# A decode layer on one core: five engine programs without a closing block

## The chip, the cores and the metric

The kernel runs on one core of a Trainium2 chip. A core has five engines with a program each: TensorE (PE, with its weight loads shown as PEld), VectorE (DVE), ScalarE (ACT), GpSimd (POOL) and SyncE (SP). [...] SyncE computes nothing here; it issues nearly all transfers (DMAs) from HBM. The metric is the time of one execution in device microseconds (us), 680.14 as the median of three runs of the kernel before.

## The reference

One token goes through one transformer layer with conditioning. `c` gives six vectors (shift, scale and gate for attention and for the feed-forward part). Attention has 32 heads of 128 over a cache of 16384 positions; K and V are read in full, 268 MB in bf16, and everything else is small beside them.

```python
mod = (_silu(c) @ w_mod).reshape(c.shape[0], 6, 1, -1)
sa, ca, ga, sb, cb, gb = ...
h = _layernorm(x) * (1 + ca) + sa
x = x + ga * A(h, k_cache, v_cache, wq, wo)      # softmax(q k / sqrt(128)) v, then wo
h = _layernorm(x) * (1 + cb) + sb
x = x + gb * B(h, w_gate, w_up, w_down)          # (silu(h wg) * (h wu)) wd
```

## The kernel before

The heads go in 16 pairs. For each pair SyncE brings 8 MB of K into one half of the ring `kring` and 8 MB of V into `vbuf`. DVE multiplies K by the query (L554, L570) and folds the products (L559, L564, L576), PE sums what is left into scores (L544, L584), DVE and PE find the largest (L589, L593, L597), ACT takes the exponential (L601), PE weighs V (L518), ACT and PE gather the output (L524, L533, L537). A half of the ring is filled again once PE has read the scores out of it, and `vbuf` once PE has read V. At the front stand the modulation vectors and the queries (L378 to L484); at the end the output projection, the second layer norm and the feed-forward part (L663 to L775), with the weights brought into freed halves of the ring.

The order of work is written out by hand. `op` and `dma` append operations to a list (`dma` is the helper at L90, so that all transfers have that line); each names its engine and the operations that it needs. `emit` goes through the list once, gives each engine its operations in the order of the list, and puts a wait ahead of an operation where its engine does not yet know that what it needs is done. The middle pairs are loops on ACT, DVE and PE (L187, L191); SyncE's and GpSimd's programs have no loop. GpSimd does two operations in all: it fills `ones_bf` (L359) and makes the identity matrix `ident` (L360) that DVE reads at L413 and PE as weights later. The last transfers are the two halves of the output row, one from SyncE and one from ACT, and SyncE's last operation is `final_wait` (L779), which needs both.

Around this stand two handshakes of all five engines. The first belongs to the set-up of every program and has the line of the launch, L813: four engines drain and raise a semaphore, GpSimd gathers the four and releases them. Then each engine goes by a branch into its own part of a block (`nc.Block`, entered at L243), and when it has reached the end of its part it goes by a branch to the block's common end. There the same handshake is made again: drain, gather by GpSimd, release. These instructions have the line L243.

Of the kernel before, what the change touches and what calls it, by code (L numbers as in the profile page):

```python
# [37 lines left out]
class _Plan:  # L38
# [38 lines left out]
    def op(self, eng, fn, deps=(), name="", chan=None):  # L77
        o = _Op(eng, fn, list(deps), name, len(self.ops), self.loop.get(eng), chan)
        o.sig = chan is not None
        self.ops.append(o)  # L80
        return o
# [20 lines left out]
                need[k] = (d.chan, d.val)  # L102
        return need

    def emit(self, block):
        for o in self.ops:
            for d in o.deps:
                d.sig = True
                assert d.seq < o.seq, (o.name, d.name)
        per_eng = {e: [o for o in self.ops if o.eng == e] for e in self.ENGS}  # L110
        for e in self.ENGS:
            by_place = {}
            for o in per_eng[e]:
                if o.loop:
                    key, i, n = o.loop
                    by_place.setdefault((key, i), []).append(o)
            for (key, i), ops in by_place.items():
                first = by_place[(key, 0)]
                assert len(first) == len(ops), (key, i)
                for a, b in zip(first, ops):  # L120
                    a.sig = a.sig or b.sig
            for (key, i), ops in by_place.items():
                for a, b in zip(by_place[(key, 0)], ops):
                    b.sig = a.sig
            for o in per_eng[e]:
                if o.sig:
                    ch = o.chan if o.chan is not None else self.chans[e]
                    o.chan = ch
                    ch.count += ch.inc
                    ch.ops.append(o)  # L130
                    o.val = ch.count

        def issue(eng, o):
            ins = o.fn(eng)
            if o.sig:
                assert ins is not None, o.name
                ins.then_inc(o.chan.sem, o.chan.inc)

        def run(name, eng):
            known = {}  # L140
            ops = per_eng[name]
            at = 0
            while at < len(ops):
                o = ops[at]
                if o.loop is None:
                    for k, (ch, v) in self.needs(o).items():
                        if known.get(k, 0) < v:
                            eng.wait_ge(ch.sem, v)
                            known[k] = v
                    issue(eng, o)  # L150
                    at += 1
                    continue
                key, i, n = o.loop
                end = at
                while end < len(ops) and ops[end].loop and ops[end].loop[0] == key:
                    end += 1
                body = (end - at) // n
                rows = [ops[at + j * body:at + (j + 1) * body] for j in range(n)]
                assert (end - at) == body * n and all(x.loop[1] == j for j, r in enumerate(rows) for x in r)
                done = {}  # L160
                body_needs = []
                for b in range(body):
                    each = [self.needs(r[b]) for r in rows]
                    assert all(set(x) == set(each[1]) for x in each[1:]), rows[0][b].name
                    for k, (ch, v) in each[0].items():
                        if k not in each[1]:

                            assert ch.ops[v // ch.inc - 1].seq < ops[at].seq, rows[0][b].name
                            if known.get(k, 0) < v:
                                eng.wait_ge(ch.sem, v)  # L170
                                known[k] = v
                    waits = []
                    for k, (ch, v1) in each[1].items():
                        step = each[2][k][1] - v1
                        v0 = v1 - step
                        assert all(x[k][1] == v0 + j * step for j, x in enumerate(each) if j), (rows[0][b].name, [x[k][1] for x in each])
                        assert v0 > 0 and step >= 0
                        assert k not in each[0] or each[0][k][1] <= v0, rows[0][b].name
                        assert v0 % ch.inc == 0 and ch.ops[v0 // ch.inc - 1].seq < rows[0][b].seq, rows[0][b].name
                        if known.get(k, 0) >= each[-1][k][1]:  # L180
                            continue
                        if k in done and done[k][1] == step and done[k][0] >= v0:
                            continue
                        done[k] = (v0, step)
                        waits.append((ch, v0, step))
                    body_needs.append(waits)
                with eng.Fori(0, n) as it:  # L187
                    self.turn = it
                    for b in range(body):
                        for ch, v0, step in body_needs[b]:  # L190
                            eng.wait_ge(ch.sem, v0 if step == 0 else it * step + v0)  # L191
                        issue(eng, rows[0][b])
                    self.turn = None
                for k, (v0, step) in done.items():
                    known[k] = max(known.get(k, 0), v0 + (n - 1) * step)
                at = end

        @block.sync
        def _(e):
            run("sp", e)  # L200

        @block.scalar
        def _(e):
            run("act", e)

        @block.vector
        def _(e):
            run("dve", e)

        @block.tensor  # L210
        def _(e):
            run("pe", e)

        @block.gpsimd
        def _(e):
            run("pool", e)


def build(nc, A_x, A_k, A_v, A_wq, A_wo, B_wg, B_wu, B_wd, c_in, w_mod, out):
# [21 lines left out]

    es = ExitStack()
    with es:  # L243
        block = es.enter_context(nc.Block())
        plan = _Plan(nc, es)
        op, dma = plan.op, plan.dma
        POOL, ACT, DVE, PE = "pool", "act", "dve", "pe"
# [529 lines left out]
        d_outs = [dma(o_dst[0:2], o_row[31:33, :], "out0", deps=[o_or], name="dma_out0"),  # L777
                  dma(o_dst[2:4], o_row[95:97, :], "out1", deps=[o_or], name="dma_out1", eng="act")]
        op("sp", lambda e: e.nop(), deps=d_outs, name="final_wait")  # L779
        plan.emit(block)  # L780
    return plan


def bass_adaLN_cond__gqa_block_cached__swiglu_ffn__decode_kernel(
    nc: bass.Bass,
    A_x: bass.AP,
    A_k_cache: bass.AP,
    A_v_cache: bass.AP,
    A_wq: bass.AP,
    A_wo: bass.AP,  # L790
    B_x: bass.AP,
    B_w_gate: bass.AP,
    B_w_up: bass.AP,
    B_w_down: bass.AP,
    c: bass.AP,
    w_mod: bass.AP,
    out: bass.AP,
):
    build(nc, A_x, A_k_cache, A_v_cache, A_wq, A_wo, B_w_gate, B_w_up, B_w_down, c, w_mod, out)
# [28 lines left out]
```

## Time and profile before

| | us |
|---|---|
| Median of three runs | 680.14 |
| Lowest, highest | 679.78, 680.22 |
| Span of the profiled execution, first to last instruction | 678.3 |
| Median less span | 1.8 |
| DVE busy | 513.5 (76%) |
| PE busy | 362.0 (53%) |
| ACT busy, POOL busy | 46.4, 0.7 |
| Transfers | 428 GB/s, 99.2% of 16 engines' span |

The page gives no time of its own for the profiled execution beside its span, so the two are compared by the median. A view by line lists an instruction's engine (a `q` behind the name is the engine's sequencer, which handles drains, semaphores and branches), its operation, how often, its least, median and greatest length in ns, and the first and last start in us from the span's start. The timeline has start, length, engine, line and operation, and in brackets how long the engine was idle before and what released it. The chain of waits is followed back from the last computing instruction or issue, in order of time. The profile starts at the first instruction of the program, the handshake of L813, and ends with the last.

### The profile page before, as it was taken

The page shows a single profiled execution, that of the slowest core. Times are in us where ns is not written, and L with a number is a line of the kernel's source. Part 1 is how long each engine was busy: PE and PEld are TensorE (multiplying, and loading weights), DVE is VectorE, ACT ScalarE, POOL GpSimd, SP SyncE. Part 2 cuts the span into 40 slices and gives each one's busy share as a digit, 9 for nine tenths or more (in the row PEclk, how much of TensorE's full clock was granted, in tenths as well). Part 3 has the DMA queues.
Part 4 walks back from the last instruction along what each step waited for, and adds up shares of the span by engine and source line. Part 5 has one row for each costly group of instructions (what it writes and reads, how often), then busy time and mean ns, then how long its engine had stood idle before and what let it go on. Part 6 is the DMA issues. An engine that isn't in the chain of part 4 may idle for free.

```text
span 678.3 us, 5380 instructions
## 1 busy us (share of the span) xinstructions
PE 362.0 (53%) x2052; PEld 143.4 (21%) x2053; DVE 513.5 (76%) x186; ACT 46.4 (7%) x146; POOL 0.7 (0%) x6
## 2 busy tenths in 40 slices
PE   2520475755728174654818375562818465471676
PEld 1110122221312122221302122121212222130235
DVE  2189997959596896959597795959698695959812
ACT  1120000100000000000000010000000000000010
POOL 0000000000000000000000000000000000000000
PEclk9675565655657565565757555575756556575775
DMA  8999999999999999999999999999999999999997
GB/s 372 443 461 429 433 437 430 433 429 433 433 429 433 437 433 433 433 433 433 433 433 433 433 433 437 433 433 433 433 433 433 433 433 433 433 433 433 433 408 304
DMA packets 6355, 290.58 MB, mean 428 GB/s; under 512 B 714, under 2 KB 972, under 8 KB 1484
## 3 DMA queue, kind: packets, MB, share of 16 engines
q1 hardware_dynamic: 6340, 290.48, 99.2%
q8 instruction: 5, 0.08, 0.0%
q14 instruction: 2, 0.02, 0.0%
q10 hardware_dynamic: 8, 0.00, 0.0%
HBM read 290.47 MB, written 0.00 MB: 428 GB/s over the span
## 4 chain that ended last, share of the span: by engine, by line
DMA 49%; DVE 30%; issue 13%; PE 8%; SPq 0%; DVEq 0%
DMA kring<-in_A_k_cache_dram 45%; DVE kring L554 10%; PE psb L544 7%; DVE kring L559 6%; DVE kring L570 5%; DVE kring L576 5%; DMA kring<-in_B_w_down_dram 4%; DVE kring L564 3%; PE psb L584 1%; SPq L90 0%; DVE pm L589 0%; DVE nb L597 0%; PE psb L765 0%; DVEq L191 0%; DVEq L554 0%
## 5 line engine op out<-in xcount | busy, mean ns | idle before, releaser
L554 DVE TENSOR_TENSOR kring<-kring,qbc 128x16384 bf16<-128x16384 bf16 x28 | 243.2, 8687 | 96.4 <-DMA kring<-in_A_k_cache_dram 96.4
L544 PE MATMUL psb<-kring,ident 128*128 x448 | 197.6, 607 | 121.3 <-DVE kring L564 121.3
L559 DVE TENSOR_TENSOR kring<-kring 128x8192 bf16<-128x8192 bf16 x28 | 123.8, 4420 | 0.5
L544 PEld LDWEIGHTS psb<-kring,ident 128*128 128x128 bf16 x448 | 54.0, 120 | 249.0 <-issue 248.3
L518 PE MATMUL psb<-vbuf,PZ 128*8 128x512 bf16 x960 | 80.4, 509 | 0.0
L593 PE MATMUL psb<-d,bd_f 128*128 128x64 f32 x32 | 10.9, 446 | 118.8 <-ACT d L591 118.8
L564 DVE TENSOR_TENSOR kring<-kring 128x4096 bf16<-128x4096 bf16 x28 | 64.0, 2286 | 0.5
L570 DVE TENSOR_TENSOR kring<-kring,qbc 128x16384 bf16<-128x16384 bf16 x4 | 34.8, 8688 | 23.4 <-DMA kring<-in_A_k_cache_dram 23.4
L518 PEld LDWEIGHTS psb<-vbuf,PZ 128*8 128x8 bf16 x960 | 26.5, 107 | 58.5 <-issue 48.6
L584 PE MATMUL psb<-kring,ident 128*128 128x128 bf16 (+1 forms) x48 | 14.3, 463 | 44.2 <-DVE kring L576 44.2
L593 PEld LDWEIGHTS psb<-d,bd_f 128*128 128x128 f32 x32 | 8.0, 311 | 121.3 <-DVE pm L589 111.6
L576 DVE TENSOR_TENSOR kring<-kring 128x8192 bf16<-128x8192 bf16 (+2 forms) x12 | 31.7, 2645 | 0.3
L533 PEld LDWEIGHTS psb<-sel,acc_sb 128*128 128x128 f32 x128 | 28.5, 310 | 8.5 <-issue 4.3
L533 PE MATMUL psb<-sel,acc_sb 128*128 128x2 f32 x128 | 25.6, 322 | 1.4 <-ACT acc_sb L524 1.4
L524 ACT ACTIVATE acc_sb<-psb 128x512 f32<-128x512 f32 x16 | 9.6, 597 | 209.7 <-PE psb L518 209.7
L601 ACT ACTIVATE PZ<-psb,nb 64x256 bf16<-64x256 f32 x32 | 15.0, 469 | 64.8 <-DVE nb L597 64.6
L584 PEld LDWEIGHTS psb<-kring,ident 128*128 128x128 bf16 x48 | 5.6, 122 | 51.8 <-DVE kring L576 44.9
L591 ACT ACTIVATE d<-negid,pm 128x64 f32<-128x64 f32 x16 | 5.6, 348 | 154.3 <-DVE pm L589 154.3
L477 PE MATMUL psb<-vbuf,h_col 128*128 128x512 bf16 x39 | 11.2, 459 | 8.3 <-DMA vbuf<-in_A_wq_dram 8.3
L537 ACT ACTIVATE OT_sb<-psb 128x2 f32 (+1 forms) x16 | 2.8, 172 | 153.3 <-PE psb L533 153.3
L589 DVE TENSOR_REDUCE pm<-psb 128x1 f32<-128x256 f32 x16 | 6.7, 418 | 3.7 <-PE psb L584 3.7
L477 PEld LDWEIGHTS psb<-vbuf,h_col 128*128 128x128 bf16 x40 | 4.3, 116 | 15.5 <-DMA vbuf<-in_A_wq_dram 8.8
(105 smaller groups left out, 77.8 us busy)
## 6 DMA issues: line engine op xcount, KB each, us to landing
kring<-in_A_k_cache_dram SPq DMA_DIRECT2D x2, 4096.0 KB, 40.1
vbuf<-in_A_wq_dram SPq DMA_DIRECT2D x1, 5120.0 KB, 25.6
kring<-in_w_mod_dram SPq DMA_DIRECT2D x1, 4800.0 KB, 14.0
vbuf<-in_A_wo_dram SPq DMA_DIRECT2D x1, 4480.0 KB, 23.3
kring<-in_B_w_gate_dram SPq DMA_DIRECT2D x1, 2160.0 KB, 18.9
kring<-in_B_w_up_dram SPq DMA_DIRECT2D x1, 2160.0 KB, 23.7
kring<-in_B_w_down_dram SPq DMA_DIRECT2D x3, 640.0 KB, 25.0
vbuf<-in_A_wo_dram SPq DMA_DIRECT2D x1, 640.0 KB, 24.5
```

The lines of the kernel that those rows point to most:

```text
L477: last = e.matmul(q_ps[b][:, 0:512], lhsT=h_col[:, k:k + 1].broadcast_to([128, 128]), rhs=wq_v[:, k, g * 512:(g + 1) * 512], start=(k == 0 ...
L518: last = e.matmul(acc_ps[32 * s:32 * s + 8, :], lhsT=PZ[:, j, :], rhs=v_at(p)[:, 4 * j:4 * j + 4, :].rearrange("p t d -> p (t d)"), start= ...
L533: last = e.matmul(OT_ps[:, 0:2], lhsT=acc_sb[:, 128 * i:128 * (i + 1)], rhs=sel[:, i:8:4], start=(i == 0), stop=(i == 3))
L544: last = e.matmul(S_ps[:, 0:T2], lhsT=ident[:], rhs=kring[:, bass.ds(plan.slot(p), 1), :, d].rearrange("p o t -> p (o t)"), start=(d == 0) ...
L554: return e.tensor_tensor(out=kv4, in0=kv4, in1=q4, op=ALU.mult)
L559: o_f = op(DVE, lambda e: e.tensor_tensor(out=kv4[:, :, 0], in0=kv4[:, :, 0], in1=kv4[:, :, 1], op=ALU.add), deps=[o_m], name="fold%d_%d" ...
L564: return op(DVE, lambda e: e.tensor_tensor(out=lo[:, :, 0:QR], in0=lo[:, :, 0:QR], in1=lo[:, :, QR:QW], op=ALU.add), deps=[o_f], name="fol ...
L570: o = op(DVE, lambda e: e.tensor_tensor(out=kv, in0=kv, in1=qbc[:, p, :].unsqueeze(1).broadcast_to([128, KCUT[c + 1] - KCUT[c], 128]), op= ...
L576: o = op(DVE, lambda e, w=w: e.tensor_tensor(out=kv[:, :, 0:w], in0=kv[:, :, 0:w], in1=kv[:, :, w:2 * w], op=ALU.add), deps=[o], name="fol ...
L584: last = e.matmul(S_ps[:, a:b], lhsT=ident[:], rhs=kring[:, p % 2, a:b, d], start=(d == 0), stop=(d == 15))
L593: o_mx[p] = op(PE, lambda e: e.matmul(mx_ps[:, 0:64], lhsT=bd_f[:], rhs=d2[:], start=True, stop=True), deps=[o_d2, o_bd1, o_bd2, o_nb[p - ...
L601: o_exp[p] = op(ACT, lambda e, half=half, ps=ps: e.activation(out=PZ[ps, :, 4 * half:4 * half + 4], in_=S_ps[ps, 0:T2].rearrange("p (c i) ...
```

## The change

The block is no longer entered. SyncE's and GpSimd's operations are put straight into the main program, behind the first handshake. ACT, DVE and PE, whose programs have loops, are sent from the main program by a branch each into a body of their own, which stands alone and has no common end. With the block go its closing drain, gather and release on all five engines, and the branches to it. The waits and operations that `emit` makes for each engine are the same, in the same order, `final_wait` among them. All lines behind the edits stand 11 lines higher in the file after.

```diff
-    def emit(self, block):
+    def emit(self):
...
-        @block.sync
-        def _(e):
-            run("sp", e)
-
-        @block.scalar
-        def _(e):
-            run("act", e)
-
-        @block.vector
-        def _(e):
-            run("dve", e)
-
-        @block.tensor
-        def _(e):
-            run("pe", e)
-
-        @block.gpsimd
-        def _(e):
-            run("pool", e)
+        nc = self.nc
+        run("sp", nc.sync)
+        run("pool", nc.gpsimd)
+        looped = [(nc.scalar, "act"), (nc.vector, "dve"), (nc.tensor, "pe")]
+        for eng, name in looped:
+            nc.br("go_" + name, engines=[eng.engine])
+        for eng, name in looped:
+            with nc.body("go_" + name, valid_engines=[eng.engine]):
+                run(name, eng)
...
-        block = es.enter_context(nc.Block())
...
-        plan.emit(block)
+        plan.emit()
```

## The prediction

> **What bounds the kernel now.** I read the page first (shares, slices, queues), then the chain of waits in order of time, and last the instructions that the closing handshake itself left, line by line. The header and the first rows give the frame:
>
> ```profile
> span 678.3 us, 5380 instructions
> ...
> PE 362.0 (53%) x2052; PEld 143.4 (21%) x2053; DVE 513.5 (76%) x186; ACT 46.4 (7%) x146; POOL 0.7 (0%) x6
> ...
> DMA  8999999999999999999999999999999999999997
> ...
> q1 hardware_dynamic: 6340, 290.48, 99.2%
> q8 instruction: 5, 0.08, 0.0%
> q14 instruction: 2, 0.02, 0.0%
> HBM read 290.47 MB, written 0.00 MB: 428 GB/s over the span
> ```
>
> The reader is to see that no compute engine is full, that the transfers of queue 1 are (99.2% of what 16 engines can take), and that the two queues which carry instructions took no measurable share. The stream of K, V and weights from HBM sets the length, so between its first issue and its last landing an edit that issues no transfer and holds none up is worth nothing. What is left to win lies before the first issue and behind the last landing. The timeline and the chain show both ends:
>
> ```profile
> 0.74 0.07 issue
> ...
> 0.80 0.40 SPq L90 DMA_DIRECT2D kring<-in_w_mod_dram  x1
> ...
> 648.87 26.02 DMA kring<-in_B_w_down_dram
> 674.89 0.04 issue
> 674.94 1.06 PE psb L765 x21
> 676.00 0.02 issue
> 676.02 0.34 DVE qbc L774
> 676.36 0.02 issue
> 676.38 0.24 DVE o_row L775
> ...
> 676.65 0.33 SPq L90 DMA_DIRECT2D out_dram<-o_row  x1
> 676.66 0.26 ACTq L90 DMA_DIRECT2D out_dram<-o_row  x1
> ```
>
> The first columns are start and length in us. The last weights land at 674.9, the output row is ready at 676.6, its two halves are issued at 676.65. Everything after that is waiting for the output to land and the handshake. The instructions of the lines concerned follow (length in ns as least, median and most, then first and last start in us); L779 is the final wait, L243 the block whose end makes the handshake, L813 the handshake before the program:
>
> ```profile
> L779 SPq EVENT_SEMAPHORE  x1: 17/17/17, 677.8 to 677.8; - x1
> ...
> L243 POOLq EVENT_SEMAPHORE  x2: 17/17/17, 678.1 to 678.2; - x2
> L243 POOLq DRAIN  x1: 387/387/387, 1.0 to 1.0; - x1
> L243 PEldq DRAIN  x1: 363/363/363, 675.7 to 675.7; - x1
> L243 DVEq DRAIN  x1: 280/280/280, 676.4 to 676.4; - x1
> L243 ACTq DRAIN  x1: 241/241/241, 677.0 to 677.0; - x1
> L243 SPq COMPARE_BRANCH  x1: 33/33/33, 678.0 to 678.0; - x1
> L243 SPq DRAIN  x1: 7/7/7, 678.1 to 678.1; - x1
> L243 SPq EVENT_SEMAPHORE  x1: 17/17/17, 678.3 to 678.3; - x1
> L243 ACTq EVENT_SEMAPHORE  x1: 17/17/17, 678.3 to 678.3; - x1
> L243 DVEq EVENT_SEMAPHORE  x1: 21/21/21, 678.3 to 678.3; - x1
> L243 PEldq EVENT_SEMAPHORE  x1: 51/51/51, 678.3 to 678.3; - x1
> ...
> SPq L779 <- DMA out_dram<-o_row: 0.8, 1, 0.8
> SPq L243 <- PEq L243: 0.2, 1, 0.2
> ```
>
> Four engines drain while others still work or the output is in flight (1.0, 675.7, 676.4 and 677.0), so their drains cost nothing today. On the path are only SyncE's branch at 678.0, its drain, GpSimd's two semaphore instructions and the four releases at 678.3: the 0.2 us in the last row is SyncE's wait for the release.
>
> **The change, part by part.** The sum is made against this execution, whose page gives a span of 678.3; its own time is not listed. The median of the three runs is 680.14 (679.78 to 680.22), so 1.8 us of a run lie outside the span, and I carry them as a separate term.
>
> *The closing handshake goes.* Removed are five drains, GpSimd's gather and go and four releases, 11 instructions, and the branches to the common end. Of these the path holds the stretch from 678.0 to the end of the span: 678.3 - 678.0 = 0.3 us. With the rounding of both rows it is 0.25 to 0.4. What is late next: the landing of the output. SyncE waits for two semaphores at L779; one instruction of 17 ns is shown at 677.8 and then nothing of SyncE until the branch at 678.0. Either the branch carries the second wait and the 0.2 us are the other half of the output still in flight, or they are the way to the branch. In the first case they stay (the new program waits for both semaphores in one instruction, which would start at about 678.0); in the second they go too, and the gain is 0.5. I take the first: the two halves leave within 0.01 us of each other on two queues, but the branch is 33 ns long and no row shows SyncE needing 0.2 us from one control instruction to the next (its first issue follows the opening release by 0.07). So -0.3, between -0.25 and -0.5.
>
> *SyncE's and GpSimd's programs stand in the main program.* No DMA, no wait and no operation changes its order on any engine; set side by side, the two instruction lists differ on SyncE in the branch in and the branch out, on GpSimd the same. SyncE's transfers and GpSimd's memset and select are issued in the order they had. What can move is the way into the program:
>
> ```profile
> L813 SPq EVENT_SEMAPHORE  x1: 17/17/17, 0.7 to 0.7; - x1
> ...
> 0.80 1.28 ACT L353 ACT_TABLE_LOAD   x1 [0.80 <-PEq L813]
> 0.80 0.20 POOL L359 MEMSET ones_bf<- 128x128 bf16 x1 [0.29 <-POOLq L813]
> ...
> 0.87 0.09 DVE L363 MEMSET rl<- 1x32 f32 x1 [0.87 <-PEq L813]
> ...
> 1.07 0.29 POOL L360 TENSOR_SCALAR_AFFINE_SELECT ident<-ones_bf 128x128 bf16<-128x128 bf16 x1
> ...
> 10.95 0.22 DVE L413 TENSOR_TENSOR negid<-ident 128x64 f32<-128x64 bf16 x1
> ```
>
> SyncE is released at 0.74 and issues at 0.80. No branch instruction of L198 to L214 left a row, on any engine, so either it is laid out as a fall through or hides in these 0.07 us. Since SyncE's first issue starts the stream that sets the length, what it gains there counts in full: 0 to 0.07 earlier. I take 0: GpSimd, ACT and DVE, released by the same handshake, start at 0.80, 0.80 and 0.87, so SyncE is already as quick as any. [...] GpSimd's program may start that much earlier too: its mask is first read by DVE at 10.95, 9.6 us after its last instruction (1.07 + 0.29), so it is covered, and would cost its delay only beyond that.
>
> *The other three get bodies of their own.* They branch into a body as they branched into the block, so the entry (0.80 on ACT, 0.87 on DVE) costs what it did: 0, with the same 0.07 as the bound either way. The instructions of ACT, DVE and PE are then one place further forward or back in their code. If that moved a code load into a loop of PE, the stall would fall where the transfers cover it: a K transfer takes 38.7 us from issue to landing (the chain's rows of about 38.7 per pair) while queue 1 stays full, because it queues behind the V transfer; and PE stands idle before its rows of L544 for 121.3 us in all, waiting for DVE, so that most of a late start would be waiting time today. Cover gone, that is in the last 30 us, it would cost its own length once.
>
> ```profile
> 337.89 38.72 DMA kring<-in_A_k_cache_dram
> ...
> L544 PE MATMUL psb<-kring,ident 128*128 x448 | 197.6, 607 | 121.3 <-DVE kring L564 121.3
> ```
>
> *The 1.8 us outside the span.* No row shows them. Bounded from both sides by what is known of them: if they are the common end of the run, PE, ACT, DVE and GpSimd may now go through their shares early, since GpSimd is done at 1.4, PE at 676.0, DVE at 676.6 and ACT at about 677.2, and only SyncE's share is left behind 678.0; at the most all 1.8 go. If instead that end is made longer by engines arriving apart, it could at the most be had twice, +1.8, on the reading that each end is walked through once by the early four and once for SyncE. I take 0, which is what the nearest row says: GpSimd waits in the handshake from 1.4 to 678.1, and answers SyncE's drain within 0.1 us, so an engine that came early by 677 us was neither quicker nor slower to let the others go. [...]
>
> The sum: 680.14 - 0.3 + 0 + 0 + 0 = 679.8. Its ends by the terms inside the span: 680.14 - 0.5 - 0.07 = 679.6 and 680.14 - 0.25 + 0.07 = 680.0.
>
> **The rivals.**
> 1. *The end outside the span shrinks as well.* For: SyncE's control instructions take 17 ns, PE's 51 (the last two rows of L243), three times as much; if PE's share is what makes the 1.8 us, and PE now works it off from 676.0, then SyncE's share of about 1.8 x 17 / 51 = 0.6 is left and 1.2 go. [...] Time: 680.14 - 0.3 - 1.2 = 678.6, at the most 680.14 - 0.5 - 1.8 = 677.8. It decides from 1.06 us gained outside (1.36, which is 0.2% of 680, less 0.3).
> 2. *The end outside the span grows*: with no common release the engines come to it up to 677 us apart, and it is walked through once early and once more for SyncE. For: only that the handshake made all five start it within 0.1 us (SyncE's and PE's rows at 678.3). Against: GpSimd's early arrival costs nothing in the handshake. Time: 680.14 - 0.3 + 1.8 = 681.6; it decides from 1.7 us more (1.36 + 0.3).
> 3. *The change does not do what it says*: another release of all five is put at the end in place of this one. Then 680.14 - 0.1 to 680.14, say 680.1. For: the final instructions of the three bodies end without a branch and something must follow. Against: the instruction list ends on SyncE with the two waits and no drain.
>
> **How the numbers follow.** The forecast (only the stretch in the span goes) has a chance of 0.58, rival 3 has 0.05, rival 1 has 0.27, rival 2 has 0.10. A bound of 0.2%, 1.36 us, is about what a measurement of this kernel can tell from no change; 679.8 and 680.1 lie within it, so same is 0.63, faster 0.27 and slower 0.10. The likeliest one's own range is 679.6 to 680.0, and with the spread of the three runs (0.4) 679.4 to 680.3. To leave out no more than 2 in 10, the range reaches down over the 678.6 of rival 1 to 678.4, where about 0.08 of it is left out, and up to 680.4, the forecast's end with the same spread, which leaves rival 2 out: 678.4 to 680.4.
>
> **What would show it.** Right: no drain and no release behind the output's landing on any engine; SyncE's last instruction at about 678.0 is the end of the span; the span is 0.3 shorter with SyncE's first issue still at 0.80; the share of queue 1 stays at 99%; time less span stays at 1.8. Wrong: time less span moves by 1 us or more (rivals 1 and 2 by its sign), a drain after 677 on several engines (rival 3), the 0.2 us between SyncE's two final waits gone (the larger gain in the span), a first issue away from 0.80, or a code load in a loop with instruction queues that carry more than 5 and 2 packets. What makes the prediction wrong above all is the term that no row shows.

## The result and the profile after

The changed kernel takes 679.24 us (median of 21 runs, 678.91 to 679.48) against 680.10 of the kernel before (21 runs, 679.77 to 680.48): a ratio of 0.9987 with a 95% interval of 0.9981 to 0.9993. It is faster by 0.86 us, 0.13%, inside the 0.2% that the prediction counted as no change, and about three times the 0.3 us that it worked out.

The page of the kernel after has these rows for the frame:

```profile
span 677.8 us, 5368 instructions
...
PE 365.1 (54%) x2052; PEld 143.7 (21%) x2053; DVE 513.6 (76%) x186; ACT 46.4 (7%) x146; POOL 0.7 (0%) x6
...
DMA  9999999999999999999999999999999999999997
...
q1 hardware_dynamic: 6340, 290.48, 99.3%
q8 instruction: 5, 0.08, 0.0%
q14 instruction: 2, 0.02, 0.0%
```

Twelve instructions are gone (5380 to 5368): five drains, two of GpSimd's, four releases and SyncE's branch. The counts of computing instructions, the transfers and the packets of the instruction queues are the same. The two ends of the span, by the timeline of the kernel after:

```profile
0.80 0.20 POOL L348 MEMSET ones_bf<- 128x128 bf16 x1 [0.29 <-POOLq L802]
0.80 0.40 SPq L90 DMA_DIRECT2D kring<-in_w_mod_dram  x1
...
676.23 0.24 DVE L764 TENSOR_TENSOR o_row<-qbc 128x160 bf16<-128x160 bf16 x1
676.50 0.33 SPq L90 DMA_DIRECT2D out_dram<-o_row  x1
676.50 0.26 ACTq L90 DMA_DIRECT2D out_dram<-o_row  x1
```

The first issue is at 0.80, where it was. What follows the last one is a single row, here with SyncE's wait for the output from the view of waits:

```profile
L768 SPq EVENT_SEMAPHORE  x1: 28/28/28, 677.8 to 677.8; - x1
...
SPq L768 <- DMA out_dram<-o_row: 1.0, 1, 1.0
```

One instruction now waits for both halves and starts 1.3 us after the issue (677.8 less 676.50), just as the branch did before (678.0 less 676.65). In the trace of the kernel before, the instruction at L779 waits for the semaphore of ACT's half and the branch for that of SyncE's half, so the 0.2 us between them were the second half in flight, and they stay.

The profiled execution took 679.08 us, 1.3 more than its span, where the prediction had counted on 1.8. The record lists each run's own span beside its time for the 21 runs of the kernel after and for the 81 runs of the kernel before that were taken beside the experiments below (not for the 21 above). Over these both parts can be averaged, and the second lies in a narrow band:

| | mean span | time less span, mean (lowest to highest) |
|---|---|---|
| before, 81 runs | 678.33 | 1.76 (1.69 to 1.88) |
| after, 21 runs | 677.95 | 1.28 (1.21 to 1.38) |
| difference | -0.38 | -0.48 |

The bands of the second column do not touch. More than half of the gain lies outside the span, in the term that no row shows. The runs of the two rows were not taken side by side; the first experiment, which was taken beside 33 of the 81, gives the same two differences (-0.37 and -0.50).

### The profile page after: what moved, and what is told of

Its sections match the earlier page's. It is cut to its first block, busy times and chain, and to the rows that moved or that the text cites. A ratio compares the mean times of both kernels' runs of the same rounds, so it can differ in the third digit from the quotient of the medians.

```text
span 677.8 us, 5368 instructions
## 1 busy us (share of the span) xinstructions
PE 365.1 (54%) x2052; PEld 143.7 (21%) x2053; DVE 513.6 (76%) x186; ACT 46.4 (7%) x146; POOL 0.7 (0%) x6
## 4 chain that ended last, share of the span: by engine, by line
DMA 45%; DVE 30%; issue 13%; PE 11%; ACT 0%; DVEq 0%; SPq 0%
DMA kring<-in_A_k_cache_dram 45%; DVE kring L543 10%; PE psb L533 7%; DVE kring L548 6%; DVE kring L559 5%; DVE kring L565 5%; DVE kring L553 3%; PE psb L507 1%; PE psb L712 1%; PE psb L675 1%; PE psb L573 1%; PE psb L687 0%; PE psb L754 0%; DVE pm L578 0%; DVE nb L586 0%
## 5 line engine op out<-in xcount | busy, mean ns | idle before, releaser
L507 PE MATMUL psb<-vbuf,PZ 128*8 128x512 bf16 x960 | 83.1, 521 | 0.0
L466 PE MATMUL psb<-vbuf,h_col 128*128 128x512 bf16 x39 | 9.8, 415 | 8.3 <-DMA vbuf<-in_A_wq_dram 8.3
```

What stands on the lines that cost most here:

```text
L466: last = e.matmul(q_ps[b][:, 0:512], lhsT=h_col[:, k:k + 1].broadcast_to([128, 128]), rhs=wq_v[:, k, g * 512:(g + 1) * 512], start=(k == 0 ...
L507: last = e.matmul(acc_ps[32 * s:32 * s + 8, :], lhsT=PZ[:, j, :], rhs=v_at(p)[:, 4 * j:4 * j + 4, :].rearrange("p t d -> p (t d)"), start= ...
```

## The experiments

Theory A: the part outside the span holds each engine's own way out of the program, and the time ends with the last of them; the handshake sent all five out together, behind the output, and now only SyncE leaves that late. This is read from the times alone, since no row shows an engine's way out. The rivals are B, that the gain outside comes from SyncE's and GpSimd's programs standing in the main program; C, that a handshake leaves something to do behind the span, whoever comes when; and D, that the part grows with the number of engines that come late. The measure is time less span. Its bands are about 0.2 wide, while the intervals of the ratios are about as wide as the whole effect; spans are listed to 0.1, so a mean of time less span over 11 runs is good to a few hundredths, and a mean span, which varies more, to about 0.1. The kernel before itself gives 1.78, 1.75 and 1.77 in the three groups of its 81 runs, so differences under 0.05 are not read as anything.

**All five in bodies.**

```diff
-        run("sp", nc.sync)
-        run("pool", nc.gpsimd)
-        looped = [(nc.scalar, "act"), (nc.vector, "dve"), (nc.tensor, "pe")]
+        looped = [(nc.sync, "sp"), (nc.gpsimd, "pool"), (nc.scalar, "act"), (nc.vector, "dve"), (nc.tensor, "pe")]
```

> SyncE and GpSimd get bodies of their own too, as the other three have; there is still no closing handshake. Theory A (the time outside the span shrank from 1.8 to 1.27 us because four engines now reach their end before SyncE does) expects the time of the changed kernel: 679.2, span 678.0, time less span 1.27. Theory B (it shrank because SyncE's and GpSimd's programs stand in the main program) expects time less span 1.8 and a time of 679.8.

Measured: 679.15 us, ratio to the kernel before 0.9988 (0.9979 to 0.9997), mean span 677.95, time less span 1.28 (1.22 to 1.38). B falls: where the programs of SyncE and GpSimd stand is worth nothing. SyncE's first issue with a body, by its timeline, is at 0.80 again:

```profile
0.80 0.40 SPq L90 DMA_DIRECT2D kring<-in_w_mod_dram  x1
```

**A handshake put back.**

```diff
+        came, go = (self.es.enter_context(nc.semaphore(n)) for n in ("came", "go"))
+
+        def close(name, eng):
+            if name == "pool":
+                eng.wait_ge(came, 4)
+                eng.nop().then_inc(go, 1)
+                return
+            eng.drain().then_inc(came, 1)
+            eng.wait_ge(go, 1)
+            eng.nop()
         run("sp", nc.sync)
+        close("sp", nc.sync)
         run("pool", nc.gpsimd)
+        close("pool", nc.gpsimd)
...
                 run(name, eng)
+                close(name, eng)
```

> The changed kernel with a handshake of five engines put back at its end by hand: four drains, GpSimd's gather and its release; SyncE's and GpSimd's programs stay in the main program. Theory A expects 680.1 again, as the kernel before: span 678.3, time less span 1.8, since the release lets all five go at once. Theory B expects the span of before with the new outside part, 678.3 + 1.27 = 679.6. Theory C (the handshake's own instructions leave something to do behind the span, whoever comes when) expects 680.1 like A.

Measured: 679.86 us, ratio 0.9996 (0.9987 to 1.0005), mean span 678.09, time less span 1.77 (1.70 to 1.86). The part outside is back at its old size. The time misses A's 680.1, because the span is 0.24 shorter than with the block: this form has no branch with the last wait on it (the drain carries it; in the block the drain starts 0.16 behind the branch) and one instruction of GpSimd for gather and release (in the block two, 0.08 apart). The rows by line show it (L206 is the drain, L204 GpSimd's, L208 the wait for the release):

```profile
L204 POOLq EVENT_SEMAPHORE  x1: 17/17/17, 678.0 to 678.0; - x1
...
L206 PEldq DRAIN  x1: 273/273/273, 675.8 to 675.8; - x1
...
L206 SPq DRAIN  x1: 7/7/7, 678.0 to 678.0; - x1
...
L208 PEldq EVENT_SEMAPHORE  x1: 51/51/51, 678.0 to 678.0; - x1
```

**No handshake, but all five late.**

```diff
         op("sp", lambda e: e.nop(), deps=d_outs, name="final_wait")
+        for late in ('pe', 'act', 'dve', 'pool'):
+            op(late, lambda e: e.nop(), deps=d_outs, name="late_" + late)
```

> The changed kernel without a handshake, but PE, ACT, DVE and GpSimd each end with a wait for both halves of the output, as SyncE does: all five reach their end at about 678.0 with nothing gathered or released. Theory A expects time less span 1.8 with a span of 678.0, so 679.8. Theories B and C expect 1.27 and 679.3.

Measured: 679.87 us, ratio 0.9997 (0.9988 to 1.0006), mean span 678.02, time less span 1.80 (1.73 to 1.89). Its last rows hold no drain, no gather and no release, only five waits that start together, SyncE's at L768 and these four:

```profile
L770 ACTq EVENT_SEMAPHORE  x1: 38/38/38, 677.8 to 677.8; - x1
L770 POOLq EVENT_SEMAPHORE  x1: 43/43/43, 677.8 to 677.8; - x1
L770 DVEq EVENT_SEMAPHORE  x1: 50/50/50, 677.8 to 677.8; - x1
L770 PEldq EVENT_SEMAPHORE  x1: 51/51/51, 677.8 to 677.8; - x1
```

C falls: the extra half microsecond outside the span comes back with the late engines alone (1.80 against 1.28).

**One engine late.** PE beside SyncE first, then the final wait moved from SyncE to one other engine, so that this one alone ends behind the output:

```diff
+        op("pe", lambda e: e.nop(), deps=d_outs, name="late_pe")
```

> As the last, but only PE waits for the output beside SyncE. If theory A holds and PE's way out is the longest (its control instructions take 51 ns, SyncE's 17), time less span is 1.8 and the time 679.8, as with all four late. If another engine's way out is the longest, it stays near 1.27 and 679.3. Theories B and C expect 679.3.

```diff
-        op("sp", lambda e: e.nop(), deps=d_outs, name="final_wait")
+        op("pool", lambda e: e.nop(), deps=d_outs, name="final_wait")
```

> The changed kernel with the final wait for both halves of the output on GpSimd in place of SyncE, so that GpSimd alone ends at about 678 and SyncE ends with its last issue at 676.8. Theory A (the time outside the span is the way out of the engine that ends last; SyncE's is 1.28, PE's 1.55, the longest 1.80) expects time less span at GpSimd's own way out: 1.80 if GpSimd is the longest, another value if not, below 1.28 too if its way out is short. Theory D (it grows with the number of engines that end late, 1.28 for one and 1.80 for five) expects 1.28 for any engine alone.

> The same with the final wait on ACT. Theory A expects ACT's own way out: at least one of GpSimd, ACT and DVE has to show 1.80. Theory D expects 1.28.

> The same with the final wait on DVE. Theory A expects DVE's own way out: at least one of GpSimd, ACT and DVE has to show 1.80. Theory D expects 1.28.

> The same with the final wait on PE alone. Theory A expects 1.55, the value with PE and SyncE both late, and a time of 679.5. Theory D expects 1.28 and 679.2, since with SyncE early only one engine is late.

The last instruction of each of the last four, with the final wait on GpSimd, ACT, DVE and PE, one row per kernel from the view by line:

```profile
L768 POOLq EVENT_SEMAPHORE  x1: 43/43/43, 677.8 to 677.8; - x1
```

```profile
L768 ACTq EVENT_SEMAPHORE  x1: 38/38/38, 677.8 to 677.8; - x1
```

```profile
L768 DVEq EVENT_SEMAPHORE  x1: 50/50/50, 677.9 to 677.9; - x1
```

```profile
L768 PEldq EVENT_SEMAPHORE  x1: 51/51/51, 677.8 to 677.8; - x1
```

| last behind the output | time | ratio to before (95%) | mean span | time less span |
|---|---|---|---|---|
| SyncE (the changed kernel) | 679.24 | 0.9987 (0.9981 to 0.9993) | 677.95 | 1.28 (1.21 to 1.38) |
| DVE | 679.29 | 0.9989 (0.9980 to 0.9998) | 677.95 | 1.41 (1.31 to 1.48) |
| ACT | 679.34 | 0.9991 (0.9982 to 1.0000) | 677.93 | 1.42 (1.37 to 1.53) |
| PE | 679.52 | 0.9993 (0.9984 to 1.0002) | 678.03 | 1.52 (1.47 to 1.62) |
| PE and SyncE | 679.52 | 0.9991 (0.9982 to 1.0000) | 677.97 | 1.56 (1.47 to 1.63) |
| GpSimd | 679.82 | 0.9997 (0.9988 to 1.0006) | 678.03 | 1.82 (1.74 to 1.92) |
| all five (shown above) | 679.87 | 0.9997 (0.9988 to 1.0006) | 678.02 | 1.80 (1.73 to 1.89) |

In the five forms with one late engine the last instruction starts at 677.8 to 677.9 in the profile, and the time behind it depends on which engine that is. GpSimd alone gives what all five give, and PE alone what PE and SyncE give, within 0.05: the longest counts, not the sum or the number, so D falls. DVE and ACT are not told apart. The expectation that PE would be the longest missed, and so did both values given for PE beside SyncE (1.8, or near 1.27): it is 1.56, and GpSimd is the longest.

**A handshake without GpSimd.** `close` as above, but SyncE gathers three (`came` at 3) and releases ACT, DVE and PE, and GpSimd has no part in it:

```diff
-            if name == "pool":
-                eng.wait_ge(came, 4)
+            if name == "sp":
+                eng.wait_ge(came, 3)
...
-        close("pool", nc.gpsimd)
```

> The changed kernel with a closing handshake of four engines: ACT, DVE and PE drain and wait, SyncE gathers the three after the output has landed and releases them; GpSimd takes no part and ends at 1.4. The way outs measured with one engine last are SyncE 1.28, DVE 1.41, ACT 1.42, PE 1.52, GpSimd 1.82. Theory A expects the longest of those that take part, PE's: time less span 1.5, a span of about 678.1 (0.1 for gather and release), together 679.6. Theory C (any closing handshake costs its 1.8 behind the span) expects 679.9.

Measured: 679.59 us, ratio 0.9992 (0.9983 to 1.0001), mean span 678.05, time less span 1.55 (1.49 to 1.65): PE's way out, as A expects, and not 1.8. The trace has SyncE's gather (L203) at 677.0, ahead of the output's landing and not behind it as expected; the release still waits for the output. The last rows (L204 is SyncE's wait for the output and the release, L208 what waits for it):

```profile
L203 SPq EVENT_SEMAPHORE  x1: 17/17/17, 677.0 to 677.0; - x1
...
L204 SPq EVENT_SEMAPHORE  x1: 28/28/28, 677.7 to 677.7; - x1
...
L208 ACTq EVENT_SEMAPHORE  x1: 17/17/17, 677.8 to 677.8; - x1
L208 DVEq EVENT_SEMAPHORE  x1: 21/21/21, 677.8 to 677.8; - x1
L208 PEldq EVENT_SEMAPHORE  x1: 51/51/51, 677.8 to 677.8; - x1
```

Nothing tried beats the changed kernel beyond its spread: SyncE has the shortest way out of the five (1.28 against 1.41 to 1.82), and it already has the last wait.

## Why the prediction was right or wrong

*The closing handshake goes, -0.3.* Right in kind and nearly in size: over the runs with a listed span it is 0.38 shorter, within the 0.25 to 0.5 given. The profiled executions differ by 0.5 because the output was issued 0.15 earlier in the later one (676.50 against 676.65), which the edit does not explain. What was said to be late next, the output's second half, is.

*SyncE and GpSimd in the main program, 0.* Right: the first issue is at 0.80 in all three forms, and bodies for all five change neither part of the time (mean span 677.95, time less span 1.28, with and without them).

*Bodies for the other three, 0.* Right: ACT's table load and DVE's first memset start at 0.80 and 0.87 again, and the instruction queues carry the same 5 and 2 packets.

*The 1.8 us outside the span, taken as 0.* This is the step that failed. No run of the changed kernel shows a term of 0; it is -0.48 as a mean, and with it the sum is 680.10 - 0.38 - 0.48 = 679.24. The two bounds, -1.8 and +1.8, held it, but the value between them was chosen by the wrong row. GpSimd's wait of 677 us inside the handshake showed that an early engine releases the others promptly (its gather starts within 0.1 us of SyncE's drain); it says nothing of the time from GpSimd's own last instruction to the end, and that is 1.82 us. With the handshake GpSimd's last row of L243 starts at 678.2, and 678.2 + 1.82 gives 680.0 for a median of 680.1; PE's would give 678.3 + 1.52 = 679.8 (a time less span of 1.5, where 1.76 was measured) and SyncE's 678.3 + 1.28 = 679.6, so by these sums GpSimd's way out was the end of the kernel before. Now GpSimd is done at 1.4 and SyncE's wait at 677.8 sets the end; its 1.28 comes from these same runs, so that sum is no test of it. One engine sets the end in the runs above, and not the number of late ones, but that the early ones win nothing does not follow: the time less span fell from 1.76 to 1.28 once GpSimd, ACT, DVE and PE ended early.

That the time still fell inside 678.4 to 680.4 is owed to the width left for rival 1. The likeliest case's own range, 679.6 to 680.0, and the same with the spread of the runs, 679.4 to 680.3, do not hold 679.24, and a time less span that stays at 1.8, named as a sign of being right, did not come. One row was read slightly low, without consequence: DVE is done at 676.4 + 0.28 = 676.7, not 676.6.

*Rival 1* (the end outside shrinks) named this mechanism, with the wrong engine and the wrong scale. PE's 51 ns against SyncE's 17 promised 1.2 us; the ways out, 1.52 and 1.28, are not in that ratio, and GpSimd, whose semaphore instructions in L243 take 17 ns as SyncE's does, has the longest (1.82). At -0.48 it stayed short of the 1.06 from which it would have decided the sign. *Rival 2* (it grows) and *rival 3* (another release follows) have no trace: the part shrank, and no drain stands behind the output.

What stays open: what an engine does in its way out has no row, so it is not shown why GpSimd needs 0.5 us more than SyncE, nor how much of SyncE's 1.28 lies ahead of the span rather than behind it.

## What to carry to other kernels

Time less span is a measure of its own: compare it between versions before putting a difference down to anything in the trace, since it is far steadier here than the time itself (over the 21 runs of the kernel after it spreads over 0.17 us, the time over 0.57). Let only the engine that must wait for the output wait for it, and choose that engine: here SyncE's way out is the shortest (1.28) and GpSimd's 0.5 us longer (1.82), so the block's closing handshake cost that difference on top of its own 0.4 us. If engines must meet at the end, leave GpSimd out of it, which saved about 0.2 us of time less span here (1.77 to 1.55; the ratios to the kernel before, 0.9996 and 0.9992, have intervals too wide to show it).

## What the runs showed of the hardware

With the same last wait at the same place, the time less span was, as a mean, 1.28 us for SyncE, 1.41 for DVE, 1.42 for ACT, 1.52 for PE and 1.82 for GpSimd; with several engines late it was that of the slowest within 0.05 (1.80 for all five, 1.56 for PE and SyncE). The semaphore instructions of L243 in the kernel before, 17, 21, 17, 51 and 17 ns in the same order, do not rank the engines so: GpSimd's is as short as SyncE's. The two waits for the output, with nothing between them, were made into one instruction that took 28 ns on SyncE, 38 on ACT, 43 on GpSimd, 50 on DVE and 51 on PE.
